# Attention and a gated circular convolution on one core: nearly all products over 64 rows, in couples, with PSUM banks taken in twos

## The chip, the core and the metric

The kernel runs on one core of a Trainium2 chip. The metric is the device time of one execution, in microseconds (us). The core has a matrix engine (TensorE, PE in the profile; its weight loads are shown apart as PEld), a vector engine (DVE), a scalar engine (ACT), GpSimd (POOL), SyncE (SP), which here only issues transfers, and DMA queues. TensorE writes its results to PSUM, which this kernel uses as eight banks of 128 partitions by 512 float32 columns. Every other step reads a bank with ACT or DVE and frees it.

## What is computed

Inputs are q, k, v of 8 batches, 12 heads, 448 positions, 64 features, a projection of 768 by 2304, a filter of 448 by 768 and an output projection of 768 by 768, all float32. Cut to what matters:

```python
scores = q @ k.T / sqrt(64)
e = exp(scores - max); attn = e / (sum(e) + exp(-max) + 1e-9)    # softmax with one more zero score
x = heads side by side (attn @ v)                                # 8 x 448 x 768
x1, x2, x3 = split(x @ w_proj, 3)
x2_conv = irfft(rfft(x2, axis=1) * rfft(filter, axis=0), axis=1) # circular convolution over positions
out = (x1 * x2_conv * x3) @ w_out
```

The kernel doesn't subtract the maximum: it adds 1 to the sum of the exponentials.

## The kernel before

Operands of products are bfloat16, sums are float32 in PSUM. Heads are taken in twos: head pair `hp` of batch `b` is job `i = 6 b + hp`, 48 in all, with one head in partitions 0 to 63 and the other in 64 to 127 of `kT` and `qT`.

**Attention of one head pair** (`attention(i)`, L757). Keys come as four groups of 128. Groups 1 to 3 are ordinary (`scores(t)`, L769): for each head one product over 64 rows, the two heads side by side in the two halves of the array, into two neighbouring PSUM banks (ring `sc`). Group 0 holds the last 64 keys of both heads, zero-padded, and is one product over all 128 rows (L771). ACT takes the exponentials of two banks in one instruction of 128 x 896 (L776), of group 0 in one of 128 x 448 (L782). The values follow: `out_rests` (L791) for group 0, eight small products over 64 rows and 65 columns (the 65th column is all ones and gives the sum), and `out_rest(u)` (L799) for head `u`, twelve over 128 rows and 65 columns. `norm(u)` (L812 to L814) divides on DVE. From batch 1 on, two groups of scores are issued together (`both`), and `out_rests` of the head pair before rides behind one of these jobs (`with_rests`).

**Dense part of a batch** (`dense(b)`, L917). `P` (L973) multiplies four folded copies of the attention's output by the middle third of the projection, six products of 113 outputs by 384 columns into one bank, for four parts by two column halves. `Z` (L1000) is a transform by a small cosine and sine table, one product each. DVE multiplies by the filter's spectrum (L1014, L1020). `I` (L1085) transforms back, four products of 113 columns to a bank. `G` (L1046) makes the two gates, six products over 128 rows and 448 columns for each of six blocks and two gates; ACT copies the first gate (L1058), DVE multiplies it by the second straight from PSUM (L1061). `O` (L1158) is the output projection, six products of 384 columns for each of two column halves of a block of 128 positions; ACT copies each half (L1170), and SP stores the block (L1177). A few full 128-row transposes (L461 to L470, L893) turn inputs of the first two batches and some outputs of the attention.

**Order.** Nothing is ordered while the program runs. At build time every job is given to `Plan` with its engine, a cost, a due time, the tokens that it needs and makes, and the buffers that it takes and gives back. `Plan.run` goes through time with these costs, takes for each free engine the first ready job by due time within a window of 160, and writes the jobs out in that order; each engine then executes its list strictly in order, waiting on semaphores. `spots` (L131) gives out the eight PSUM banks: a couple of neighbouring banks for `sc`, one bank for anything else, with limits in `CAP` (L61): two couples for `sc`, two banks for `op` (values), five for `hy` (all the rest).

Of the kernel before, what the change touches and what calls it, by code (L numbers as in the profile page):

```python
# [41 lines left out]
class Plan:  # L42
# [18 lines left out]
    CAP = {"sc": 2, "op": 2, "hy": 5}  # L61
# [6 lines left out]
    def add(self, eng, cost, want, emit, need=(), make=(), take=(), give=(), dma=0.0, run=256, n=1, after=0.0, begun=(), late=0.0):  # L68
        self.tasks.append((want, len(self.tasks), eng, cost, emit, need, make, take, give, dma, after, run, n, begun, late))

    def run(self):
# [59 lines left out]
        def spots(t):  # L131

            found, count = {}, {}
            for r, tok in t[7]:
# [8 lines left out]
                if r == "sc":  # L143
                    pairs = [(max(until[i], until[i + 1]), i) for i in open_ if i % 2 == 0 and i + 1 in open_]
                    if not pairs:
                        return None
                    i = min(pairs)[1]
                    found[(r, tok)] = (i, i + 1)
                else:
                    if not open_:  # L150
                        return None
                    found[(r, tok)] = (min(open_, key=lambda i: (i < self.LOW, until[i], i)),)
# [28 lines left out]

        while any(queue.values()):
            moved = False
            for e in queue:
                if free[e] > now + 1e-9:
                    continue
                for i, t in enumerate(queue[e][: self.WINDOW]):
                    if ready(t):
                        break
                else:  # L190
                    continue
                del queue[e][i]
# [10 lines left out]
                end = free[e] = now + t[3]  # L203
# [52 lines left out]
def kernel(  # L256
# [16 lines left out]
    EARLY1 = 3.88  # L273
    ATT = [0.66, 29.26, 89.17, 109.42, 158.04, 195.13, 226.82, 281.74]
    SLOT = [2.76, 7.07, 6.79, 7.15, 3.93, 0.11, 6.90, 5.17]
    DENSE = [55.69, 86.75, 129.09, 171.42, 218.23, 260.63, 314.72, 403.09]
    PACE = [1.76, 2.25, 1.51, 1.80, 1.21, 2.06, 0.63, 0.81]
    FOLD = [-0.17, 0.59, -11.07, -14.44, 19.64, 0.57, 9.33, 0.88]
    BPS = 1.39
    RE1 = 9.47  # L280
    WT = 2.21
    FT = 18.26
    HALVED = (2,)
    AHEAD = [0, 0, 44.96, 46.56, 34, 34, 34, 34]
    LEAD = [-5.04, 8.40, 5.33, 27.02]
    LOADS = ((1, 0), (1, 1), ("F", None), (0, None), (2, None), ("O", None))
    LOAD = [36.65, 26.03, 14.30, 37.12, 39.52, 45.70]
    STEP = 3.73
    FOLD0 = (40.54, 56.31, 30.00)
# [34 lines left out]
    er = [const.tile([128, S + REM], BF16, name=f"er{i}") for i in range(2)]  # L324
# [10 lines left out]
    def stage(g, at, n):  # L335
# [6 lines left out]
            "e": 6, "er": 2, "k0": 2, "q0": 2, "u": 1, "w": 1, "xf": 1,  # L342
# [411 lines left out]

    T = {}

    def attention(i):  # L757
# [15 lines left out]
        def exps(t):  # L773
# [6 lines left out]
            else:  # L780
                P["e"][t] = e = er[i % 2]
                nc.scalar.activation(e[:, 0:S], bank(("hy", ("S", i, t)))[:, 0:S], AF.Exp, scale=SCALE)  # L782

        def out_bank(u):
            return bank(("op", (i, u)))[:, 0 : NST * (DH + 1)].rearrange("p (n d) -> p n d", n=NST)

        def out_rests():
            for n in range(NST):
                for u in range(2):
                    c = slice(64 * u, 64 * u + 64)  # L790
                    nc.tensor.matmul(  # L791
                        out_bank(u)[:, n, :], P["e"][0][c, n * 128 : n * 128 + 128], vn[b % 2][c, hp, 3, :],
# [3 lines left out]
        def out_rest(u):  # L796
            for n in range(NST):
                for t in range(3):
                    nc.tensor.matmul(  # L799
                        out_bank(u)[:, n, :],  # L800
                        P["e"][1 + t][:, u * S + n * 128 : u * S + n * 128 + 128],
                        vn[b % 2][:, hp, 4 * u + t, :],
                        start=False,
                        stop=(n == NST - 1 and t == 2),
                    )

        def norm(u):
            op = out_bank(u)
            if ("xb", b) not in W:
                W["xb", b] = xbp.tile([128, NHP, NST, 128], BF16, name="xb")  # L810
            rec = small.tile([128, NST], F32, name="rec")
            nc.vector.tensor_scalar_add(rec, op[:, :, DH], 1.0)  # L812
            nc.vector.reciprocal(rec, rec)
            nc.vector.tensor_tensor(  # L814
                W["xb", b][:, hp, :, 64 * u : 64 * u + 64],
                op[:, :, 0:DH],
                rec[:].unsqueeze(2).to_broadcast([128, NST, DH]),
# [3 lines left out]
        P["scores"], P["rests"] = scores, out_rests  # L821


        host = (2 if b == 0 or i % 2 == 0 else 3) if i else None

        def with_rests(j):
            pb = j // NHP
            vs = [("v", j), ("vr", pb)]
            return dict(
                cost=0.13, emit=T[j]["rests"], need=[("e", j), ("ones", pb % 2), "pads"] + vs, make=[("ER", j)],  # L830
                take=[("op", (j, 0)), ("op", (j, 1))], give=[("er", (j, 0))],
            )

        for t in range(4):
            w = tau(i, t / 4 if i or t else 1.0)
            ex = with_rests(i - 1) if t == host else dict(cost=0.0, emit=lambda: None, need=[], make=[], take=[], give=[])
            if t == 0 or b == 0:

                def one(t=t, ex=ex):
                    scores(t)  # L840
                    ex["emit"]()

                add("PE", (0.4 if t else 0.19) + ex["cost"], w, one,
                    need=[("kT", i), ("qT", i)] + ([("S", i - 1, 2)] if b else []) + ([] if i or t else ["kT0"]) + ex["need"]
                    + ([("S", i, t - 1) if t > 1 else ("S", i - 1, 3)] if t and (i or t > 1) else []),
                    make=[("S", i, t)] + ex["make"], take=[(ring(t), ("S", i, t))] + ex["take"], give=ex["give"])
            elif (3 * i + t) % 2 == 0:

                old = (i, t - 1) if t > 1 else (i - 1, 3)

                def both(pair=(old, (i, t)), ex=ex):
                    for j, n in pair:
                        T[j]["scores"](n)
                    ex["emit"]()

                add("PE", 0.6 + ex["cost"], tau(old[0], old[1] / 4), both,
                    need=[("kT", old[0]), ("qT", old[0]), ("kT", i), ("qT", i)] + ex["need"]
                    + [("S", old[0], old[1] - 1) if old[1] > 1 else ("S", i - 1, 3)],
                    make=[("S",) + old, ("S", i, t)] + ex["make"],
                    take=[("sc", ("S",) + old), ("sc", ("S", i, t))] + ex["take"], give=ex["give"])  # L860
            add("ACT", 0.81 if t else 0.44, w - 1.0, lambda t=t: exps(t), need=[("S", i, t)],
                make=[("e", i)], take=[("e" if t else "er", (i, t))], give=[(ring(t), ("S", i, t))])
        if i == n_batches * NHP - 1:
            ex = with_rests(i)
            add("PE", 0.19 + ex["cost"], tau(i, 1.1), out_rests, need=ex["need"], make=ex["make"], take=ex["take"],
                give=ex["give"])

        w = tau(i + 1, (2 if i % 2 else 1) / 4) + 0.01
        for u in range(2):
            add("PE", 0.385, w + 0.01 * u, lambda u=u: out_rest(u), need=[("ER", i)], make=[("V", i, u)],  # L870
                take=[("op", (i, u))], give=[("e", (i, t)) for t in range(1, 4)])
            add("DVE", 0.8, w - 0.5, lambda u=u: norm(u),
# [455 lines left out]
```

## Time and profile before

The median of three runs is 387.61 us (385.61, 387.61, 388.36). The profile is of one execution.

| of the profiled execution | |
|---|---|
| its own time | 385.59 us |
| span from first to last instruction | 383.8 us |
| granted TensorE clock, mean | 0.993 |
| TensorE matmuls | 3734 in 369.9 us busy |
| DVE | 823 instructions, 276.9 us |
| ACT | 460 instructions, 264.4 us |
| DMA | 58.74 MB, 153 GB/s mean |

The page gives each engine's busy time, the chain of work that ended last, and groups of equal instructions by line (L1046 is line 1046 of the listing). A matmul's row begins when it starts to stream and ends when its result is in PSUM, so rows of consecutive matmuls overlap: the mean of a group is a latency, and the rate is read from the distance of starts. In a timeline the columns are the start, the length of the merged stretch, the engine, the line and the shapes; a bracket tells of idle time before it and of who ended it.

### The profile page before, as it was taken

The numbers are of one execution on the slowest core, as the hardware profiler recorded it, in microseconds if no ns is written. First come the engines' busy times: TensorE is split into PE (matmuls) and PEld (weight loads), VectorE is DVE, ScalarE is ACT, GpSimd is POOL, SyncE is SP. The second block draws the span as 40 slices with busy tenths as digits, with TensorE's granted clock in tenths as the row PEclk, the third lists the DMA queues.
The fourth block names the chain that finished last, engine by engine and source line by source line (L and its number), as shares of the span: only waits on it lengthen the run. The fifth ranks groups of instructions, "written<-read, shape, count | busy, mean of one in ns | idle before, by whom it ended". The sixth has DMA issues, their size and how long they took to land.

```text
span 383.8 us, 9781 instructions
## 1 busy us (share of the span) xinstructions
PE 369.9 (96%) x3734; PEld 236.6 (62%) x3734; DVE 276.9 (72%) x823; ACT 264.4 (69%) x460; POOL 112.3 (29%) x232
## 2 busy tenths in 40 slices
PE   8979999999999999999999999999999999999995
PEld 7656665566665575665665567565675567557652
DVE  6768959955789849984499844995579656971870
ACT  5869688555876878688777777777767775543543
POOL 5678724233552643633553420100000000000000
PEclk9999999999999999999999999999999999999999
DMA  9999999999999999999999965802310042103004
GB/s 212 266 209 244 212 215 213 150 169 191 209 203 206 177 282 244 221 210 230 265 235 138 259 168 122 143 3 82 86 27 2 10 117 70 43 0 125 0 2 164
DMA packets 134574, 58.74 MB, mean 153 GB/s; under 512 B 99389, under 2 KB 130944, under 8 KB 134528
## 3 DMA queue, kind: packets, MB, share of 16 engines
q1 hardware_dynamic: 97104, 48.35, 57.3%
q0 software_dynamic: 37184, 9.54, 27.7%
q8 instruction: 29, 0.48, 0.5%
q10 hardware_dynamic: 240, 0.23, 0.3%
q14 instruction: 17, 0.14, 0.1%
HBM read 43.86 MB, written 11.01 MB: 143 GB/s over the span
## 4 chain that ended last, share of the span: by engine, by line
PE 77%; DVE 13%; DMA 4%; ACT 2%; issue 2%; POOL 1%; SPq 0%; DVEq 0%; ACTq 0%; POOLq 0%
PE psum L1046 23%; PE psum L973 14%; PE psum L1158 14%; PE psum L799 8%; PE psum L769 7%; DMA nat<-in_q_dram 2%; DVE t L1014 2%; PE psum L1000 2%; DMA nat<-in_k_dram 2%; PE psum L1085 2%; PE psum L771 2%; DVE g L1061 2%; DVE yh L1020 1%; DVE cv L1114 1%; ACT e L776 1%
## 5 line engine op out<-in xcount | busy, mean ns | idle before, releaser
L776 ACT ACTIVATE e<-psum 128x896 bf16<-128x896 f32 x144 | 126.1, 925 | 22.7 <-PE psum L769 22.6
L1046 PE MATMUL psum<-xT,wproj_bf 128*128 128x448 bf16 x576 | 121.9, 352 | 0.4 <-DVE g L1061 0.3
L1046 PEld LDWEIGHTS <-wproj_bf 128*128 128x128 bf16 x576 | 53.8, 97 | 44.5 <-issue 2.6
L973 PE MATMUL psum<-wproj_bf,xf 128*113 128x384 bf16 x384 | 69.9, 327 | 0.2 <-DVE kT L480 0.2
L973 PEld LDWEIGHTS <-xf 128*113 128x113 bf16 x384 | 49.5, 132 | 13.0 <-issue 1.4
L1158 PE MATMUL psum<-wout_bf,yT 128*128 128x384 bf16 x288 | 51.9, 327 | 1.3 <-DVE xb L814 0.5
L799 PE MATMUL psum<-vn,e 128*128 128x65 bf16 x1152 | 44.9, 195 | 0.0
L1170 ACT COPY osb<-psum 128x384 f32<-128x384 f32 x56 | 26.1, 483 | 26.8 <-PE psum L1158 26.5
L1058 ACT CAST x<-psum 128x448 bf16<-128x448 f32 x48 | 25.7, 536 | 25.3 <-PE psum L1046 25.2
L814 DVE TENSOR_TENSOR xb<-psum,rec 128x256 bf16<-128x256 f32 x96 | 40.8, 424 | 3.3
L769 PE MATMUL psum<-qT,kT 64*128 64x448 bf16 x288 | 41.4, 358 | 0.0
L799 PEld LDWEIGHTS <-e 128*128 128x128 bf16 x1152 | 39.2, 98 | 2.7
L1158 PEld LDWEIGHTS <-yT 128*128 128x128 bf16 x288 | 27.3, 98 | 21.4 <-issue 2.6
L812 DVE TENSOR_SCALAR rec<-psum 128x4 f32<-128x4 f32 x96 | 14.8, 154 | 34.5 <-PE psum L799 34.4
L598 POOL CAST vn<-nat 128x192 bf16<-128x192 f32 x72 | 27.5, 408 | 40.5 <-DMA nat<-in_v_dram 27.1
L1061 DVE TENSOR_TENSOR g<-x,psum 128x448 bf16<-128x448 bf16 x48 | 29.5, 614 | 10.6 <-PE psum L1046 9.1
L1014 DVE TENSOR_TENSOR t<-xs,hrs 113x768 bf16<-113x768 bf16 (+1 forms) x64 | 35.6, 586 | 1.6 <-ACT xs L1008 1.6
L985 DVE CAST x<-psum 113x384 bf16<-113x384 f32 x32 | 17.6, 552 | 24.8 <-PE psum L973 24.7
L532 POOL DMA_DIRECT2D nat<-in_q_dram x28 | 24.8, 888 | 29.7 <-DMA qT<-nat 17.0
L1008 ACT CAST xs<-psum 113x384 bf16<-113x384 f32 (+1 forms) x64 | 28.2, 495 | 4.1 <-PE psum L1000 3.8
L1094 ACT CAST cr<-psum 128x452 bf16<-128x452 f32 x48 | 25.3, 550 | 7.8 <-PE psum L1085 7.6
L782 ACT ACTIVATE er<-psum 128x448 bf16<-128x448 f32 x48 | 26.9, 560 | 4.4 <-PE psum L771 4.4
(109 smaller groups left out, 444.0 us busy)
## 6 DMA issues: line engine op xcount, KB each, us to landing
nat<-in_k_dram SPq DMA_DIRECT2D x48, 192.0 KB, 5.7
nat<-in_v_dram SPq DMA_DIRECT2D x48, 192.0 KB, 5.2
out_dram<-osb SPq DMA_DIRECT2D x24, 384.0 KB, 3.1
nat<-in_q_dram POOLq DMA_DIRECT2D x20, 168.0 KB, 7.6
nat<-in_q_dram SPq DMA_DIRECT2D x11, 224.0 KB, 7.5
wproj_bf<-in_moe_w_proj_dram POOLq DMA_DIRECT2D x2, 1152.0 KB, 20.4
rests<-in_k_dram SPq DMA_DIRECT2D x8, 192.0 KB, 5.3
rests<-in_v_dram SPq DMA_DIRECT2D x8, 192.0 KB, 7.0
```

The costliest lines, as they stand in the source:

```text
L598: nc.gpsimd.tensor_copy(vn[b % 2][:, hp, 4 * u : 4 * u + 3, 0:DH], sv[:, u])
L769: nc.tensor.matmul(sc[:, u, 0:S], kT[b % 2][c, hp, t, :], qT[b % 2][c, hp, :])
L776: nc.scalar.activation(e[:, 0 : 2 * S].rearrange("p (u n) -> p u n", u=2), pair(("sc", ("S", i, t)))[:, :, 0:S], AF.Exp, scale=SCALE,)
L782: nc.scalar.activation(e[:, 0:S], bank(("hy", ("S", i, t)))[:, 0:S], AF.Exp, scale=SCALE)
L799: nc.tensor.matmul(out_bank(u)[:, n, :], P["e"][1 + t][:, u * S + n * 128 : u * S + n * 128 + 128], vn[b % 2][:, hp, 4 * u + t, :], start= ...
L814: nc.vector.tensor_tensor(W["xb", b][:, hp, :, 64 * u : 64 * u + 64], op[:, :, 0:DH], rec[:].unsqueeze(2).to_broadcast([128, NST, DH]), op ...
L973: nc.tensor.matmul(pps[:FQ, :DCH], W["xf", b][:, pg, kt, 0:FQ], wproj_bf[:, kt, D + ch * DCH : D + (ch + 1) * DCH], start=(kt == 0), stop= ...
L1008: nc.scalar.copy(L["xs", par, ch][:K, pg % 2, :], L["Z", pg, ch][:K, :DCH])
L1014: nc.vector.tensor_tensor(t[:K], L["xs", par, ch][:K], h, op=ALU.mult)
L1046: nc.tensor.matmul(p[:, :S], wproj_bf[:, kt, 2 * part * D + dt * 128 : 2 * part * D + (dt + 1) * 128], xT()[:, kt, 0:S], start=(kt == 0), ...
L1061: nc.vector.tensor_tensor(g[:, dt, :], L["x1", dt], p[:, :S], op=ALU.mult)
L1158: nc.tensor.matmul(ops[:n, :DCH], y[:, dt, 0:n], wout_bf[:, dt, ch * DCH : (ch + 1) * DCH], start=(dt == 0), stop=(dt == NDT - 1),)
```

## The change

Every product over 128 rows of `P`, `Z`, `G`, `I`, `O`, of the values, and from batch 1 on of group 0 of the scores, becomes two products over 64 rows. Two outputs are made at a time, in two neighbouring banks: first the lower rows of one beside the upper rows of the other, for the whole sum (side 0), then the other way round (side 1). Side 1 adds into the banks that side 0 wrote from the other half of the array, so its first matmul waits on a semaphore that side 0's last matmul raises (`mark`, `behind`). The two sides are two jobs for the planner.

```diff
-    CAP = {"sc": 2, "op": 2, "hy": 5}
+    REACH = 9.60
+    TURN = 0.1
+    CLOSE = 0.12
+    PAIRS = ("sc", "op", "tw")
+    CAP = {"sc": 2, "op": 2, "tw": 4, "hy": 4}
...
-                if r == "sc":
+                if r in self.PAIRS:
                     pairs = [(max(until[i], until[i + 1]), i) for i in open_ if i % 2 == 0 and i + 1 in open_]
...
+                near = at = None
                 for i, t in enumerate(queue[e][: self.WINDOW]):
-                    if ready(t):
+                    if near is not None and t[0] > queue[e][near][0] + self.REACH:
                         break
-                else:
+                    if not ready(t):
+                        continue
+                    if prev is not None and t[16] in prev[6]:
+                        near = i if near is None else near
+                        continue
+                    at = i
+                    break
...
-                end = free[e] = now + t[3]
+                end = now + t[3]
+                if e == "PE":
+                    if close:
+                        end += self.CLOSE
+                    if t[15] != bool(prev and prev[15]):
+                        end += self.TURN
...
+    def mark(last):
+
+        last.then_inc(half_done, 1)
+        halves_done[0] += 1
+        tc.add_to_no_dep_group(f"half {halves_done[0]}", last.ins)
+        tc.no_tile_sem_insts.add(last.ins.name)
+        return halves_done[0]
+
+    def behind(first, count):
+
+        first.wait_op(half_done, count, "sem-ge")
...
+        def couples(units, side, part=slice(None), last=None):
+
+            first, second = units[side][part], units[1 - side][part]
+            whole = units[0]
+            for n, two in enumerate(zip(first, second)):
+                for low, (to, w, x) in enumerate(two):
+                    c = slice(64 * low, min(64 * low + 64, w.shape[0]))
+                    now = nc.tensor.matmul(
+                        to, w[c], x[c], start=(side == 0 and n == 0 and not part.start),
+                        stop=(side == 1 and n == len(whole) - 1), skip_group_check=True,
+                    )
+                    if last is not None:
+                        behind(now, last)
+                        last = None
+            return mark(now) if not side and part.stop is None else None
+
+        def twin(key, cost, w, units, need, make, extra=(), give=(), split=None):
...
+                add("PE", cost * (1.0 if split is None else (split[1], 1 - split[1])[j]), w + 0.3 * j, lambda part=part: L.update({half: couples(L[key](), 0, part)}),
+                    need=need if not j else [half + (j - 1,), *split[2]], make=[half + (j,)], take=[tw] if not j else (),
+                    row=True)
...
+            add("PE", cost, w + 0.02 + 0.3 * (len(parts) - 1), lambda: couples(L[key](), 1, last=L[half]), need=[last], make=make, give=give, row=True, apart=last)
```

`REACH` makes the planner look for another ready job to put between the two sides; where there is none it puts side 1 directly behind side 0 and counts `CLOSE` for it. `TURN` is counted where a job over 64 rows follows one over 128 or the other way round.

The rest follows from taking outputs in twos. The values of both heads are one job pair: `way` (`out_rests` and side 0) and `values(1)`; no job carries `out_rests` along any more, and no two groups of scores are tied together. `norm` takes both heads at once, group 0 of two head pairs gets one exponential of 128 x 896 (`two_exps`), and ACT copies both banks of a `Z`, an `I` and an `O` in one instruction. `P` keeps one copy by ACT and one by DVE. Both gates of a block are one twin, so the first gate's copy comes after the second side too:

```diff
-            if part == 0:
-                add("ACT", 0.43, w, lambda: gate_back(dt, 0), need=[("G", b, dt, 0)], make=[("x1", b, dt)],
-                    take=[x1], give=[hy])
...
+            tw = twin(tuple(keys), 1.135, w, lambda banks: gate(dt, banks),
...
+            add("ACT", 0.43, w, lambda: gate_back(dt, 0), need=[keys[0]], make=[("x1", b, dt)], take=[x1], give=[tw])
+            add("DVE", 0.55, w - 0.5, lambda: gate_back(dt, 1), need=[keys[1], ("x1", b, dt), "half"],
+                make=[("g", b, dt // 2)], take=[("g", b)], give=[tw, x1])
...
-        def project_back(st, ch):
-            n = 128 if st < 3 or b % 2 else REM
...
+        def project_back(st, tw):
+            L["os", st] = otp.tile([128, D], F32, name="osb")
+            nc.scalar.copy(L["os", st][:].rearrange("p (u n) -> p u n", u=2), pair(tw)[:, :, :DCH])
```

The first two blocks of `O` have side 0 in two parts, four couples that need two thirds of the gated rows and two that need the last third. The due times (`ATT`, `SLOT`, `DENSE`, `PACE`, `FOLD`, `LOAD` and others) all have new values. In the built program TensorE has 6479 matmuls in place of 3734, 6164 of them over 64 rows, where 672 were before; ACT has 364 instructions in place of 469, DVE 687 in place of 831.

## The prediction

> **What bounds the kernel now.** I read the page first, then the waits, then timelines of TensorE.
>
> ```profile
> PE 369.9 (96%) x3734; PEld 236.6 (62%) x3734; DVE 276.9 (72%) x823; ACT 264.4 (69%) x460; POOL 112.3 (29%) x232
> ...
> PE 77%; DVE 13%; DMA 4%; ACT 2%; issue 2%; POOL 1%; SPq 0%; DVEq 0%; ACTq 0%; POOLq 0%
> ```
>
> TensorE is busy nearly throughout and carries 77% of the chain that ended last, so time is won or lost on TensorE. Its busy figure hides short holes, since a row lasts until its result has landed. So I take rates from starts. The timeline of TensorE inside batches 4 and 5:
>
> ```profile
> 240.04 0.55 PE L769 MATMUL psum<-qT,kT 64*128 64x448 bf16 x4
> 240.43 0.28 PE L791 MATMUL psum<-vn,er 64*128 64x65 bf16 x8
> 240.64 1.19 PE L973 MATMUL psum<-wproj_bf,xf 128*113 128x384 bf16 x6
> 241.66 0.92 PE L799 MATMUL psum<-vn,e 128*128 128x65 bf16 x24
> ...
> 244.92 0.49 PE L1000 MATMUL psum<-x,ft 113*112 113x384 bf16 x2
> 245.25 1.30 PE L1046 MATMUL psum<-xT,wproj_bf 128*128 128x448 bf16 x6
> 246.38 0.35 PE L771 MATMUL psum<-qT,kT 128*128 128x448 bf16 x1
> 246.57 2.43 PE L1046 MATMUL psum<-xT,wproj_bf 128*128 128x448 bf16 x12
> 248.94 0.55 PE L769 MATMUL psum<-qT,kT 64*128 64x448 bf16 x4
> ```
>
> Three things are to be seen. (a) Full rows: 245.25 to 246.38 is six matmuls of 448 columns, 0.189 each; 244.92 to 245.25 is two of 384, 0.163 each. (b) Half rows in couples: four L769 take 0.39, so a couple costs 0.195, the same as one full matmul and not twice it. Eight L791 take 0.21, which with the next point leaves 0.12, or 0.030 a couple; 24 full ones of L799 take 0.76, or 0.032 each. (c) Changing the height costs: 246.57 to 248.94 is 2.37 for twelve matmuls that need 12 x 0.189 = 2.27, so 0.10 is lost before the 64-row scores. The other way, L791's four couples need 0.12 of their 0.21, so 0.09 is lost. The first 128-row matmul after it can lose a little more for a weight load that nothing hid: six L973 take 1.02 where 6 x 0.162 = 0.97 is due.
>
> Real stalls are few. The waits of TensorE:
>
> ```profile
> PE psum L893 <- DVE xb L814: 1.7, 2, 1.0
> PE psum L463 <- POOL k L421: 1.7, 1, 1.7
> PE psum L1085 <- DVE xb L814: 1.1, 2, 0.9
> ```
>
> These are the largest, totals in us. By start distances I count about 13 us of stalls: 6.6 in the first 43 us and 6.4 after.
>
> **What the change takes away.** Streaming stays as it is: a couple of 64-row matmuls does the work of one 128-row matmul at the same rate (b), with twice the instructions. Counted in the order of the two programs, changes of height fall from 160 to 71, because transposes, the filter's spectrum and batch 0's group 0 stay full. 89 x 0.096 (mean of 0.10 and 0.09) is 8.5 us, and some forty hidden weight loads of 0.01 to 0.05 make it **-9 us**. Small values at 0.030 and not 0.032 give 1152 x 0.001, **-1 us**. DVE loses 48 of 96 sets of small reciprocal steps, and ACT a quarter of its instructions; both have slack (72% and 69%), so I give that nothing. Were TensorE quicker than them in a stage, it would be worth at most the 6.4 us of stalls.
>
> **What it adds: TensorE waits for itself.** Each of 233 second sides waits until the last matmul of its first side has landed. Queued behind it is everything that TensorE does next, so the wait can't be stepped around. No such wait exists in the trace, so I price it by two neighbours. A row's latency beyond its streaming:
>
> ```profile
> L1046 PE MATMUL psum<-xT,wproj_bf 128*128 128x448 bf16 x576 | 121.9, 352 | 0.4 <-DVE g L1061 0.3
> ...
> L973 PE MATMUL psum<-wproj_bf,xf 128*113 128x384 bf16 x384 | 69.9, 327 | 0.2 <-DVE kT L480 0.2
> ```
>
> 352 - 189 and 327 - 162 give 0.164. A hop on a semaphore: DVE's L1061 ends at 212.68 and the L1046 that waits for it starts at 212.74, 0.05 to 0.06; from TensorE to ACT, L1158's stretch ends at 379.35 and the copy starts at 379.38, 0.03. So side 1 starts 0.19 to 0.22 after side 0 has stopped streaming; I take 0.216, as the hop that ends at TensorE is the nearest. What lies between the sides in the program's order pays for it. Summing the pitches of the matmuls in between: 34 second sides have nothing between them and their first, 34 x 0.216 = 7.3 us; 116 have one short job, 0.184 on average, mostly one couple of scores or of `Z`, 116 x 0.032 = 3.7; 83 have more and lose nothing. That makes **+11 us**. It is steep: at 0.18 it is 6.6 us, at 0.25 it is 16. The floor is that of a change of height, 0.096, which also waits for the array to empty: 3.3 us. After a wait that bites, the partner's weight load is exposed, 0.01 as after the stall at 64.61 (next start 0.067 on, not 0.056) to 0.05: 150 of them, **+1 us** (0 to 5).
>
> **Banks in twos.** Eight single banks become four couples. An exponential holds its couple for 0.35 (the matmul) + 0.03 + 0.925 + 0.05 = 1.36 us from the start of the scores. In the new order 36 places give a bank back to TensorE with less matmul work in between than such a chain needs, 7.8 us short in sum (3.3 of it in batch 5, where scores follow each other closely); the same count for the order before gives 2 places and 0.35 us. The self-waits stretch the same distances, so I take less than half, **+3 us**, with 0 and 8 as ends.
>
> **The end.** The last stage runs on DVE's chain; TensorE then works off `O`:
>
> ```profile
> 371.05 2.11 PE L1158 MATMUL psum<-wout_bf,yT 128*128 128x384 bf16 x12
> 373.32 2.12 PE L1158 MATMUL psum<-wout_bf,yT 128*128 128x384 bf16 x12 [0.15 <-DVE yT L1129]
> ```
>
> After the last gate TensorE has twelve matmuls of 0.162 in hand, then waits 0.3 for DVE, then 36 more. Changed, it has 8 couples (1.30) in hand, while the first gate's copy (0.53, earlier done one matmul group sooner), the multiply (0.61) and `yT` (0.55) with three hops must pass: about 2.0. After that 40 couples are left where 36 matmuls were, 0.65 more, and the last copy is of 768 columns, some 0.3 more than the 0.48 of 384. The earlier return of 0.3 set against this, **+1 us** (0.5 to 3).
>
> **Sum.** 385.6 - 9 - 1 + 11 + 1 + 3 + 1 = 391.6 on the profiled execution's own time. The median of the runs lies 2.0 above that execution, so the forecast is **394 us**.
>
> A rule that speaks against the change, beside the row: couples of L791 start 0.030 apart, so 65 columns over 64 rows cost no more than over 128. The Trainium skill (TensorEngine Tiling (Array Packing), Instruction Overhead) gives each matmul about 60 cycles of overhead and advises against tiling where a dimension is already small; at its 2.4 GHz that would be an estimated 0.025 per matmul, hence 0.050 a couple, and with 28 couples for each of 48 head pairs some 27 us more. The row decides, so the sum has none of it; but it shows only eight in a row, where the change issues up to 32.
>
> **Rivals.**
>
> *Faster: the self-wait is cheap.* If the array's emptying is all that side 1 waits for (0.096, 3.3 us in sum), and the other engines' lighter load makes up for banks in twos: 385.6 - 9 - 1 + 3.3 + 1 = 380, or 382 as a median. For it: four sides in five have something between them, and a change of height empties the array in 0.096. Against it: a semaphore has to go out and back, and every hop in the trace takes 0.03 or more after a row's end at 0.164. The change breaks even when waits, banks and end together cost 10 us, which is at about 0.17 a wait. Chance 0.27.
>
> *Slower: banks in twos rule.* If the bank shortfall comes in full (8) and the self-waits and the end at their upper values (16, 5 and 3): 385.6 - 10 + 32 = 408 at the worst, some 403 with half of the excess. Chance 0.12.
>
> *Slower: instructions come too slowly.* Weight loads and matmuls are 12,958 where 7468 were. The densest long stretches of the trace, near 8 to 25 us, bring 256 matmuls in 17.3 us, which shows no more than one per 0.068 sustained; shorter bursts reach one per 0.031 over 32. If 0.031 were the limit for the values' 2688 matmuls, they would take 83 us where 40 are due; with half of it covered by instructions queued ahead, +20 us, so 414. The trace has no hole that looks like it. The Trainium skill (TensorE: Matmul & The Clock Gate, Wait — 56ns, not 53.3ns?) states about 62 ns of microcode per matmul where hardware decode is off; 6479 of these would be an estimated 402 us by themselves, and no run here shows which setting holds. Chance 0.08.
>
> *It doesn't do what it says: couples that add into PSUM don't run side by side.* L769 writes without adding; L791 adds only over 65 columns. If couples of 384 and 448 columns went one after the other, some 290 us of streaming would double. Chance 0.03.
>
> **How the numbers follow.** The forecast's own case, 388 to 400, has 0.50. One per cent of 387.6, about what a measurement can tell, sets the bounds 383.7 and 391.5. Faster: three quarters of the first rival and a tail of the forecast, 0.22. Same: the rest of that rival and over a quarter of the forecast, 0.21. Slower: 0.57. The range 381 to 406 leaves out some 0.08 at the faster end and 0.12 above.
>
> **What would show it.** In the changed profile a couple of 448 columns starts every 0.19 and one of 65 every 0.030 (else the last two rivals). Side 1's first matmul, directly behind side 0's last, starts about 0.40 after it with 448 columns (0.189 + 0.216); 0.29 would speak for the cheap wait. Changes of height lose 0.09 to 0.10 at 71 places. Waits of TensorE on ACT's L814 (exponentials) would show the banks, and `yT` the end. I am wrong if starts keep step through the second sides, or if stalls in the first 43 us, which I left as they are, move by several us.

## The result and the profile after

The changed kernel takes 407.81 us (median of four runs, 405.21 to 416.09) where the kernel before takes 387.84 (385.61 to 388.36). The ratio is 1.051, with a 95% interval of 1.045 to 1.057: slower by 20 us. The forecast was 394 with a range up to 406. The execution first profiled was a disturbed one (416.09 us, mean granted clock 0.970), so the lines below are from a second execution of the same kernel: 411.47 us, span 409.6, clock 0.984. They lie some 4 us above the median. Below, a self-wait is the wait of a side 1 for its own side 0, and a hole is a stretch in which TensorE stands still.

From the page of the changed kernel: busy time of the engines, the granted clock in 40 slices, the queue that brings TensorE its instructions (packets, MB, share), and the chain that ended last:

```profile
PE 377.3 (92%) x6479; PEld 266.8 (65%) x6479; DVE 261.1 (64%) x679; ACT 259.6 (63%) x355; POOL 111.3 (27%) x231
...
PEclk9996999999999999999999899999999999999998
...
q8 instruction: 50, 0.82, 0.9%
...
PE 71%; DMA 10%; DVE 10%; ACT 3%; issue 3%; POOL 1%; SPq 1%; ACTq 0%; DVEq 0%; POOLq 0%
```

TensorE is busy for 7 us more, but its share falls from 96% to 92%: the time went mostly into idle time of the engine that bounds the kernel. DMA carries 10% of the chain where it carried 4%. The line of q8 has its counterpart on the page of before, which the prediction didn't look at:

```profile
q8 instruction: 29, 0.48, 0.5%
```

The groups of `G` and of the values in the changed kernel (line, engine, shapes, count, busy and mean ns, idle before):

```profile
L1021 PE MATMUL psum<-xT,wproj_bf 64*128 64x448 bf16 x1152 | 125.3, 351 | 0.8 <-ACT er L822 0.4
...
L846 PE MATMUL psum<-vn,e 64*128 64x65 bf16 x2304 | 54.7, 191 | 2.2 <-issue 1.4
```

1152 matmuls over 64 rows are busy for 125.3 us where 576 over 128 rows took 121.9. Couples do run side by side, and streaming costs what it did. The timeline of TensorE late in the attention, beside which the first timeline of before can be read:

```profile
227.66 0.37 PE L807 MATMUL psum<-qT,kT 64*128 64x448 bf16 x2
227.90 0.36 PE L874 MATMUL psum<-qT,kT 64*128 64x448 bf16 x2
228.08 0.36 PE L807 MATMUL psum<-qT,kT 64*128 64x448 bf16 x2
228.27 0.19 PE L834 MATMUL psum<-vn,er 64*128 64x65 bf16 x1
228.92 0.27 PE L834 MATMUL psum<-vn,er 64*128 64x65 bf16 x6 [0.46 <-DVE g L1133]
232.00 0.20 PE L834 MATMUL psum<-vn,er 64*128 64x65 bf16 x1 [2.81 <-issue]
232.00 0.58 PE L846 MATMUL psum<-vn,e 64*128 64x65 bf16 x24
232.39 0.38 PE L807 MATMUL psum<-qT,kT 64*128 64x448 bf16 x2
```

Couples of scores start 0.18 to 0.24 apart, as forecast; 24 small values stream in 0.39. But TensorE stands still for 2.81 us in the middle of eight small products of one job, and no semaphore released it: "issue". No such line was among the largest waits of before. Those of the changed kernel (TensorE's line, who released it, total us, times, longest):

```profile
PE psum L937 <- DVE xb L864: 3.6, 2, 3.4
PE psum L834 <- issue: 2.8, 1, 2.8
PE psum L492 <- POOL q L449: 2.1, 4, 0.9
PE psum L483 <- DVE xb L864: 1.8, 1, 1.8
PE psum L1021 <- issue: 1.6, 2, 0.8
PE psum L846 <- issue: 1.4, 2, 0.9
PE psum L807 <- ACT x L1063: 1.4, 1, 1.4
PE psum L834 <- ACT e L814: 1.3, 2, 0.7
PE psum L1021 <- DVE yT L1196: 1.3, 1, 1.3
```

The self-waits aren't in this list at all: a start 0.22 after the end of streaming leaves only 0.06 of idle time behind the row before, whose latency reaches 351 - 189 = 0.16 beyond its streaming. They must be taken from starts. The end of the kernel shows one:

```profile
391.79 2.69 PE L1021 MATMUL psum<-xT,wproj_bf 64*128 64x448 bf16 x24
394.29 1.48 PE L1021 MATMUL psum<-wout_bf,yT 64*128 64x384 bf16 x16
397.05 2.77 PE L1021 MATMUL psum<-wout_bf,yT 64*128 64x384 bf16 x32 [1.28 <-DVE yT L1196]
```

391.79 to 394.29 is 2.50 for twelve couples, and 12 x 0.189 = 2.27; the 0.23 left is side 1 of a gate, directly behind its side 0.

Going through all start distances of TensorE in this way, with everything beyond the streaming put down to its cause, gives (us; a self-wait bites where TensorE really stood for it):

| lost by TensorE | before (span 383.8) | after (span 409.6) | difference |
|---|---|---|---|
| changes of height, 160 and 71 | 15.3 | 6.8 | -8.5 |
| self-waits that bite, 137 | 0 | 13.5 | +13.5 |
| no releaser | 0.4 | 7.9 | +7.5 |
| waiting for ACT | 0.4 | 7.9 | +7.5 |
| waiting for DVE | 8.8 | 10.2 | +1.4 |
| waiting itself for a transfer (`kT`, `xT`) | 0 | 1.5 | +1.5 |
| from the last matmul's start to the end | 4.8 | 6.2 | +1.4 |
| spread over many small differences | | | +1.5 |
| span | 383.8 | 409.6 | +25.8 |

Of the 10.2 for DVE, 3.4 is one wait at 31.55 us: DVE, which works in order, had stood idle for 4.1 us until the filter's transfer (`filt`) landed, and the `xb` that TensorE needed came behind that. In the kernel before, DVE never waited for `filt`.

**The holes without a releaser.** Counting TensorE's instructions, weight loads among them, in the order of their starts, six holes after 50 us stand at nearly the same place of a block of 256: at numbers that leave 190, 186, 184, 182, 182 and 180 when divided by 256 (the count is good to about 2). Five are "issue". The first of the six, at 57.11, is the 1.4 us under `ACT x L1063` above, since that semaphore had come shortly before. Queue q8 brings packets of 16 KB, 50 of them for 12,958 instructions: one packet is 256 instructions. Late in the kernel, with few transfers left, packets start when TensorE is near instruction 160 of a block (0.6 us before it to 1.4 after), so the boundary at which a packet is asked for is put there. Three of the holes with their packets (worked out from the trace's start and length of each packet; us):

```
boundary before passed   packet starts   packet landed   TensorE goes on   hole
186.40                   190.85          192.01          193.30            0.9
200.56                   205.08          206.17          207.62            1.0
221.97                   228.60          230.38          232.00            2.8
```

A packet is asked for when TensorE passes the boundary before, starts with a delay while other transfers run, takes about 1.2 us, and TensorE goes on 1.3 to 1.7 us after it has landed, in all six holes. In the kernel before, between 50 and 250 us, packets start 2.6 us after the boundary on average, at most 4.0, and blocks of 256 instructions last 12.5 us (median; the shortest 10.2), so every packet landed at least 6.5 us before the next boundary. In the changed kernel, in the same stretch, blocks last 7.4 us (the shortest 3.9), and packets start 3.8 us after the boundary on average, up to 7.0. The six holes cost 7.6 us. The wait at 31.55 stands near the same place in its block, but its packet had landed at 26.61, so it isn't one of them.

### The profile page after: what moved, and what is told of

Same layout as the page of the kernel before. It is cut to its first block, busy times and chain, and to the rows that moved or that the text cites. A ratio compares the mean times of both kernels' runs of the same rounds, so it can differ in the third digit from the quotient of the medians.

```text
span 414.2 us, 14970 instructions
## 1 busy us (share of the span) xinstructions
PE 382.5 (92%) x6479; PEld 270.9 (65%) x6479; DVE 261.7 (63%) x679; ACT 259.8 (63%) x355; POOL 112.1 (27%) x231
## 4 chain that ended last, share of the span: by engine, by line
PE 72%; DMA 9%; ACT 7%; DVE 6%; issue 4%; POOL 1%; SPq 1%; DVEq 0%; ACTq 0%; POOLq 0%
PE psum L1021 53%; PE psum L846 7%; PE psum L807 5%; ACT e L814 4%; DMA filt<-in_moe_filter_fft_dram 2%; DMA xT<-xb 2%; DMA kT<-nat 2%; DMA nat<-in_v_dram 2%; PE psum L874 2%; PE psum L834 1%; DMA nat<-in_k_dram 1%; DVE cv L1181 1%; PE psum L1288 1%; PE psum L937 1%; DVE g L1133 1%
## 5 line engine op out<-in xcount | busy, mean ns | idle before, releaser
L1021 PE MATMUL psum<-xT,wproj_bf 64*128 64x448 bf16 x1152 | 128.9, 358 | 0.2
L1021 PEld LDWEIGHTS <-wproj_bf 64*128 64x128 bf16 x1152 | 66.2, 96 | 40.4 <-issue 6.6
L1021 PE MATMUL psum<-wproj_bf,xf 64*113 64x384 bf16 x768 | 73.5, 324 | 0.9 <-issue 0.5
L1021 PEld LDWEIGHTS <-xf 64*113 64x113 bf16 x768 | 57.7, 128 | 9.9 <-issue 2.7
L846 PE MATMUL psum<-vn,e 64*128 64x65 bf16 x2304 | 56.2, 194 | 7.3 <-issue 6.6
L1021 PE MATMUL psum<-wout_bf,yT 64*128 64x384 bf16 x576 | 54.6, 323 | 1.4 <-DVE yT L1196 1.3
L846 PEld LDWEIGHTS <-e 64*128 64x128 bf16 x2304 | 46.9, 96 | 13.4 <-issue 10.2
L1021 PEld LDWEIGHTS <-yT 64*128 64x128 bf16 x576 | 31.0, 94 | 17.4 <-DVE yT L1196 2.0
L864 DVE TENSOR_TENSOR xb<-psum,rec 128x512 bf16<-128x512 f32 x48 | 33.2, 691 | 1.7
L1082 ACT CAST xs<-psum 113x768 bf16<-113x768 f32 (+1 forms) x32 | 24.9, 803 | 5.7 <-PE psum L1021 3.3
```

What stands on the lines that cost most here:

```text
L846: now = nc.tensor.matmul(out_bank(u)[:, n, :], P["e"][1 + t][c, u * S + n * 128 : u * S + n * 128 + 128], vn[b % 2][c, hp, 4 * u + t, :], ...
L864: nc.vector.tensor_tensor(W["xb", b][:, hp].rearrange("p n (u d) -> p u n d", u=2), op[:, :, :, 0:DH], rec[:].unsqueeze(3).to_broadcast([1 ...
L1021: now = nc.tensor.matmul(to, w[c], x[c], start=(side == 0 and n == 0 and not part.start), stop=(side == 1 and n == len(whole) - 1), skip_g ...
L1082: nc.scalar.copy(L["xs", par, ch][:K], pair(tw)[:K, :, :DCH])
```

## Experiments

Two theories were open. One: TensorE waits for its instructions, which is a rival that the prediction priced as a rate of issue and not as late packets. The other: banks in twos and the new order starve TensorE through ACT and DVE. The self-wait was common to both.

**A second execution of the changed kernel**, unchanged.

> The changed kernel once more, for a second trace. If the holes without a releaser come from TensorE running out of fetched instructions, they stand again before instructions whose number is 180 to 184 modulo 256, while transfers are busy (before 250 us), each about 1.5 us after a packet of 16 KB has landed, though not all at the same blocks. If they were chance disturbances of that one execution (clock 0.97), this one, at about 405 to 408 us, has none. Second sides directly behind first ones start 0.40 us after the last 448-column matmul in either case.

411.47 us, the profile shown above. Which boundaries are late differs between executions: the execution first profiled has its holes of over 2 us at 31.89, 198.32 and 229.90, this one at 232.00. The place in the block stays (178 to 190), and in the first execution too TensorE goes on 1.2 to 1.7 us after the packet has landed, at seven holes with 10 us of idle time. That execution has one more long wait, of 4.3 us, for DVE's gate: DVE had waited for the transfer `xT<-xb`, which landed 8.4 us after its issue.

**No self-waits.** Side 1 takes the same halves as side 0, so each sum holds one half of its rows twice and the other not at all:

```diff
-            first, second = units[side][part], units[1 - side][part]
+            first, second = units[0][part], units[1][part]
...
-                        behind(now, last)
...
-                        u = low ^ side
+                        u = low
```

> Side 1 takes the same halves as side 0 (each output adds the same 64 rows twice, so values differ from the reference), and nothing waits on its own first side; order, instructions, streaming and banks stay. If the self-waits cost what the trace shows (139 of them, 13.8 us), it takes 407.8 - 14 = 394 us, 392 to 397. If they only cover waits for banks or for instructions that come late, those grow in their place and it takes 400 to 406. If self-waits were the whole loss, it would be at or below 388.

403.11 us (398.61 to 404.48), ratio 1.041 (1.034 to 1.049). So 4.7 us of the 13.5 came back. Its profile has 8.3 us without a releaser, and waits for DVE have grown from 10.2 to 14.6. Of these, 4.7 is one wait behind `xT<-xb`, at the same instruction as in the first execution of the changed kernel, so it can't be put down to the edit. That a self-wait that is taken away lets TensorE reach the next late packet or late buffer sooner fits the numbers, but isn't separated here from such differences between executions.

**More instructions in the kernel before.** The products of `G`, `P` and `O` are cut into columns, four quarters (7622 matmuls) or two halves (5030), all over 128 rows, with no self-wait and the old order and banks:

```diff
-                nc.tensor.matmul(
-                    p[:, :S],
+                for z in range(4):
+                    zs = slice(z * (S // 4), (z + 1) * (S // 4))
+                    nc.tensor.matmul(
+                        p[:, zs],
```

> The kernel before with every matmul of G, P and O cut into four of a quarter of the columns: 7622 matmuls in place of 3734, no second sides, no banks in twos, the same order. 3888 more starts at 0.0025 us add 10 us of streaming, so 398 if the number of instructions costs nothing else. If instruction fetch binds while transfers are busy, holes at block boundaries come on top, 3 to 10 us: 401 to 408, all of them before 250 us.

> As the one with quarters, but halves: 5030 matmuls, 1296 more starts, 3 us of streaming, 391 us. With 9.8 us to a block of 256 instructions on average the fetch should still keep up: no hole, or one or two of under 1 us. If holes are as many as with quarters, it is not the rate of instructions that makes them.

Halves: 390.61 us in one execution, no hole at a boundary. Quarters: 409.63 (407.88 to 412.54), ratio 1.062 (1.055 to 1.069). That looks like a proof of the first theory and isn't one. The page of the quarters, with the weight loads of `P` (L975) and `O` (L1164), and the largest wait without a releaser:

```profile
PE 393.7 (97%) x7622; PEld 354.5 (87%) x7622; DVE 276.4 (68%) x823; ACT 264.8 (65%) x460; POOL 114.2 (28%) x232
...
q8 instruction: 59, 0.97, 1.0%
...
L975 PEld LDWEIGHTS <-xf 128*113 128x113 bf16 x1536 | 86.8, 134 | 2.9 <-issue 1.1
...
L1164 PEld LDWEIGHTS <-yT 128*128 128x128 bf16 x1152 | 51.1, 98 | 4.2 <-issue 3.4
```

```profile
PE psum L1164 <- issue: 1.3, 3, 0.9
```

TensorE's share is 97% and holes at boundaries sum to about 2 us, in spite of 59 packets. The time went into the matmuls: a quarter of `O` (96 columns) starts every 0.042 and one of `G` (112) every 0.049, near a quarter of 0.162 and 0.189, but one of `P` (96) only every 0.053. `P` alone has weights of 113 columns, and their loads are the longer ones (134 ns against 98); 96 columns no longer hide them. 1536 x (0.053 - 0.0405) is 19 us, and `G` and `O` add 2304 x 0.002 + 1152 x 0.0015 = 6: all of the excess, where about 10 had been allowed. The Trainium skill (TensorE: Matmul & The Clock Gate, Weight-path perf modes) has its fast weight load only for weights of 128 columns, which agrees with 134 against 98. Packets alone don't stall TensorE: here, between 50 and 250 us, blocks last 6.5 us, never under 5.4, and packets start at most 5.8 after the boundary. It takes short blocks together with late packets.

**Quiet queues.** If other traffic makes the packets late, less of it should bring them in time. The transposing transfers of q and k of batches 2 to 7 are left out, in the changed kernel and in the one before (their scores then use the operands of batches 0 and 1 again; `k_turn` is emptied like `q_turn`):

```diff
         def q_turn(gs=gs, st=st):
-            nc.sync.dma_start(
-                qT[b % 2][:, gs, st * SP : (st + 1) * SP], qn[:, st, 128 * gs.start : 128 * gs.stop], transpose=True
-            )
+            pass
```

> The changed kernel with the same transfers left out. If late instruction fetch behind busy DMA queues costs what the two traces show after 60 us (6 to 7 us of holes at block boundaries, 1 to 3 us of halved clock behind the long ones, 1 us waiting for kT), it takes 396 to 400 us and has no such hole after 60 us. If the holes only stand where TensorE would otherwise wait for banks or DVE, it stays at 404 to 408 with longer waits on ACT and DVE.

> The kernel before without the 28 and 16 transposing transfers of q and k of batches 2 to 7 (these batches' scores use what batches 0 and 1 left in qT and kT); everything else stays. TensorE has no hole at a block boundary here and hardly waits for transfers, so every theory expects 383 to 387 us, within 1% of the kernel before.

Changed: 399.93 us (398.61 to 402.92), ratio 1.033 (1.024 to 1.041). Before: 384.13 (382.83 to 386.77), 0.995 (0.991 to 0.998). The changed kernel gains 7.9 by the medians (7.0 by the ratios), the kernel before 2.3 against its 386.39 in the same comparison (2.1 by the ratio). The page of the changed kernel without these transfers, and a stretch like the one of the 2.81 us hole:

```profile
q1 hardware_dynamic: 61136, 39.50, 37.6%
q0 software_dynamic: 37184, 9.54, 24.4%
q8 instruction: 50, 0.82, 0.8%
```

```profile
221.08 0.50 PE L828 MATMUL psum<-vn,er 64*128 64x65 bf16 x8
221.41 0.55 PE L840 MATMUL psum<-vn,e 64*128 64x65 bf16 x24
221.93 0.36 PE L801 MATMUL psum<-qT,kT 64*128 64x448 bf16 x2
222.12 0.56 PE L840 MATMUL psum<-vn,e 64*128 64x65 bf16 x24
222.74 0.37 PE L801 MATMUL psum<-qT,kT 64*128 64x448 bf16 x2
```

Still 50 packets, but q1 has 61,136 packets in place of 97,104. Between 50 and 250 us instruction packets start 2.0 us after the boundary on average in place of 3.8, and after 60 us no hole behind a late packet is left; three before that remain, 3.5 us of idle time. The eight small products that were torn apart run through in 0.33. The same instructions, in the same order, no longer stall there: this settles that the holes after 60 us are packets held up by other transfers. It doesn't settle how much of the 7.9 is theirs. The idle time behind late packets falls from 7.2 to 3.5 us between the two profiles, but TensorE's own wait for `kT` (1.1) goes as well, and DVE waits 1.9 us for `xT<-xb` in place of 8.9.

**Quiet queues and no self-waits**, the two edits together.

> As the one before, and side 1 takes the same halves as side 0 without a wait (each output adds the same 64 rows twice). If fetch and self-waits add up (10 and 4.7 us), 392 to 395 us. What is then left over the kernel before is banks in twos and the order. If the two hide each other, 397 to 403.

390.09 us (388.68 to 393.08), ratio 1.009 (1.005 to 1.014). Now the self-waits are worth 9.8 us (from 399.93), twice what they were with busy queues. And 6.0 are left over the kernel before with quiet queues (384.13), though this one changes height 89 times less. Its waits:

```profile
PE psum L483 <- DVE xb L854: 2.6, 1, 2.6
PE psum L801 <- ACT e L808: 2.1, 6, 0.6
PE psum L1006 <- DVE g L1115: 2.0, 2, 1.0
PE psum L828 <- ACT e L808: 1.6, 3, 0.7
```

By start distances TensorE waits 11.2 us for ACT and 11.8 for DVE, 23.0 in all. With quiet queues the kernel before waits 10.3 for DVE and next to nothing for ACT. 8.5 gained on height, some 13 given back at the other engines and about 1.5 at the end make the 6.0.

**The new order and banks, with products over 128 rows again.** Jobs, order, banks and ACT's and DVE's work are the changed kernel's; side 0 makes one output, side 1 the other, each over all rows:

```diff
-            first, second = units[side][part], units[1 - side][part]
...
+            for n, (to, w, x) in enumerate(units[side][part]):
+                nc.tensor.matmul(to, w, x, ...)
```

> The changed kernel's order and banks in twos, but every product of the change again over 128 rows (side 0 makes one output, side 1 the other, no self-wait): 3733 matmuls, 336 changes of height in place of 71, 25 us more. Without self-waits (4.7) and fetch holes (12 in all) it takes 407.8 - 16.7 + 25.4 = 416 us, with no hole at a block boundary. If the number of instructions had no part in the holes, 428. If banks in twos and the order cost nothing, it is the kernel before plus 176 changes of height: 403.

409.04 us in one execution, span 407.2. It has as few instructions as before and no self-wait, and no hole at a boundary after 20 us:

```profile
PE 390.4 (96%) x3733; PEld 237.4 (58%) x3733; DVE 260.2 (64%) x679; ACT 259.1 (64%) x355; POOL 112.2 (28%) x231
...
q8 instruction: 29, 0.48, 0.5%
```

```profile
PE psum L926 <- DVE xb L857: 2.3, 2, 2.1
PE psum L1006 <- DVE yT L1178: 1.3, 1, 1.3
```

Its 23.4 us over before come apart as 16.9 for 176 more changes of height (336 x 0.096 = 32.2), 2.8 more waiting for ACT and DVE (12.0 in place of 9.2), 1.4 more at the end, and 2.3 left, which the clock can account for: it was near half speed from about 33 to 41 us, and its mean allows up to 3.8 ((1 - 0.984) x 407.2 against (1 - 0.993) x 383.8). So the order and the banks cost little while TensorE is slow, in this one execution; the 13 us of the run with quiet queues and no self-waits appear when it is quick.

**Shorter exponentials.** If the exponentials held the banks for too long, halving them should free TensorE. From batch 1 on, the exponential covers one bank of its two, so the other head's weights stay stale; with quiet queues, in the kernel without self-waits and in the one before:

```diff
+                m = 2 if b == 0 else 1
...
-                    e[:, 0 : 2 * S].rearrange("p (u n) -> p u n", u=2), pair(("sc", ("S", i, t)))[:, :, 0:S], AF.Exp,
+                    e[:, 0 : m * S].rearrange("p (u n) -> p u n", u=m), pair(("sc", ("S", i, t)))[:, 0:m, 0:S], AF.Exp,
```

> The run with transposes left out and both sides alike, and from batch 1 on each exponential of two banks does only the first (448 of 896 columns; the other half keeps an older head pair's values). Its couple of banks comes back 0.37 us sooner. If what is left over the kernel before (390.1 against 384.1) stands where scores wait for exponentials, the 11 us of waits on ACT shrink to under 3 and it takes 380 to 383. If it is the fixed order and DVE, 388 to 390.

> The same halved exponentials in the kernel before with the transposes left out. TensorE waits on ACT for under 1 us there, so all theories expect 383 to 385 us, as without the halving (384.1). A gain of several us would say that the exponentials bind in both kernels, and the run beside this one shows nothing of banks in twos.

387.69 us (386.8 to 392.2), ratio 1.003 (0.998 to 1.007), and 383.07 (382.76 to 384.69), 0.992 (0.987 to 0.997). The gap shrinks from 6.0 to 4.6. TensorE's waits for ACT fall from 11.2 to 6.6, but those for DVE rise from 11.8 to 12.7. The 1.4 between 6.0 and 4.6 is within the intervals of the four ratios (about 2 us each), so that exponentials explain any of the 6 isn't shown; the hoped-for larger share didn't come.

**More between the sides.** The planner lets a side 1 be ready only 0.23 us after its side 0, so that it looks harder for something to put in between:

```diff
+            if len(t) > 16 and t[16] in when and when[t[16]][0] + 0.23 > now + 1e-9:
+                return False
```

> The changed kernel, computing everything, but the planner holds a second side ready only 0.23 us after its first side's end, so it puts more work in between or counts the wait. By the order, 64 second sides fall short and not 150, by 4.7 us and not 11. Were self-waits additive, it would gain 6 us: 402. Since leaving all of them out gained 4.7 with transfers running, I expect 403 to 406, holes at block boundaries as before. Above 408 the new order costs more than the waits.

410.90 us (407.43 to 416.37), ratio 1.059 (1.050 to 1.067). Self-waits fall from 13.5 to 5.8 us, as meant, and the kernel is no faster: waits for ACT go from 7.9 to 15.0, for DVE from 10.2 to 17.4. What was put between the sides seems to have been taken from where it was needed.

**Fewer changes of height without any couples.** In the kernel before, the planner prefers a ready job of the same height among those due within 3 us:

```diff
+                    if e == "PE" and t[15] != prev:
+                        near = i if near is None else near
+                        continue
```

> The kernel before, products as they were; only the planner, when TensorE comes free, prefers a ready job of the same height whose due time is within 3 us of the first ready one's. Changes of height fall from 160 to 150: 10 x 0.096 = 1 us, so 385.5 beside 386.5, if the changed order costs nothing. A loss of over 1 us would say that the order written with these due times has no slack for even that.

392.39 us (390.52 to 394.51), ratio 1.013 (1.008 to 1.018): ten changes fewer (about 1 us) and 5 us more in all. The waits:

```profile
PE psum L1059 <- DVE xb L827: 2.9, 2, 2.5
PE psum L782 <- DVE xT L915: 2.1, 1, 2.1
PE psum L483 <- POOL q L440: 1.6, 3, 0.8
PE psum L1059 <- DVE g L1074: 1.6, 1, 1.6
```

Waits for DVE are 15.4 us in place of 8.8. The order of before had no slack for this rearrangement.

No kernel tried computes everything and beats the one before.

## Why the prediction was wrong

**What held.** The sign, and the sizes of what TensorE does by itself. Couples of 448 columns start 0.189 apart, of 384 every 0.162: they run side by side, and the rival that they don't is out. Changes of height fell to 71 at 0.092 to 0.096 each, -8.5 us (-9 forecast). A side 1 directly behind its side 0 starts 0.216 to 0.220 after the end of streaming, and 0.406 after its last start with 448 columns, where 0.216 and about 0.40 were forecast from a row's latency and a hop. That ruled out the cheap self-wait (0.096), the most likely rival. 137 self-waits bite and cost 13.5, the exposed weight loads with them, where 150 at 11 + 1 were forecast; the spread of what lies between the sides is a little less kind than the count by the planner's order. Small couples start 0.0315 apart, so the values gain nothing (-1 forecast), and the rule of 60 cycles overhead per matmul is not borne out either: it would have shown 0.050. The same couples, two matmuls in 0.0315, leave no room for the 62 ns of microcode for each that the prediction quotes; it said that no run shows which setting holds, but its own row of 0.030 a couple already did.

**The step that failed** is in the third rival: "The trace has no hole that looks like it." It took slow instructions as a rate of issue and looked for that rate in the densest bursts. TensorE issues fast enough; it runs out of instructions at the end of a block of 256 when the next packet is late. No hole was to be seen in the trace of before because after 50 us packets came 6.5 us early or more, and before that still 2.1. But the margin could be read there: 29 packets on q8, how late each started (up to 4.0 us), and how long the shortest blocks lasted (10.2, and 8.0 in the first 50 us). Halving these puts a block of 4 to 5 us against a packet that needs up to 4.0 + 1.1 + 1.4 = 6.5. In the changed kernel packets even started up to 7.0 late; why later than before stays open. The missing term measured 7.6 us at six boundaries. With it the sum of 391.6 on the profiled execution would have been about 399. Late packets can also cost clock: it is at half speed for 3.4 us from 232.8, right after the longest hole, worth at most 1.7 us. The clock's mean allows 3.8 us more loss than before in all, but the other halved stretches, at 31.4 and 38.2 us, go with waits for DVE.

The Trainium skill (Runtime: NRT & Kernel Launch, Instruction fetch mechanics) says that instructions come in blocks of 16 KiB, 256 of them, which the sequencer fetches through a DMA queue of its own while it executes the current block, and that the cost is "mostly hidden". The packets of 16 KB agree. Hidden holds for the kernel before and, after 60 us, for the quiet one, and not for the changed one with busy queues, where one crossing cost 2.8 us. The same skill (TensorE: Matmul & The Clock Gate, What's actually happening) halves the clock after at least one idle window of about 3.4 us. The halved stretches in the profiles of both kernels do last 3.4 us, but no wholly idle window came before them: in the 3.4 us before the one at 232.8 TensorE was busy for 0.8 us, and in the kernel before, ahead of one at 27.2, for 1.8.

**Banks in twos, and the order, under-sized.** +3 was forecast (0 to 8). TensorE waits 18.1 us for ACT and DVE where it waited 9.2, and 1.5 of that is a late packet under ACT's name: +7.4. Not all of this is banks. 3.4 is the wait behind `filt` at 31.55, which leaves +4.0; with it stalls in the first 43 us are about 9.3 in this profile where they were 6.3, a sign of being wrong that the prediction had named. DVE also stood idle for `xT<-xb` for 8.9 us where it stood 0.5 before, and how much of that TensorE's waits for DVE hold isn't separated. The count behind the 3 looked at which banks come back late, and "I take less than half" because self-waits stretch the distances. That reason fits the run with 128-row products, where TensorE is slow too and the waits grow by 2.8. The miss was to treat the term as its own. What TensorE saves elsewhere makes it meet ACT and DVE sooner. When self-waits and most late packets are gone the same waits grow to 23.0, so part of the savings is spent there. How the 6.0 us left then divide between the exponentials' hold on the banks, the banks of the rest and the fixed order stays open, as no kernel had the one without the other.

**The end**, +1 forecast: TensorE stands about 1.1 us longer for `yT` (by starts 1.46 in place of 0.32, counted above with DVE), and the last matmul's start lies 1.4 further from the end. That is about +2.5, inside the 0.5 to 3.

**What wasn't costed** and is small: TensorE's own waits for transfers, 1.5 us, nearly all of it `DMA kT<-nat` at one place.

The forecast sum, -9 - 1 + 11 + 1 + 3 + 1 = +6, becomes -8.5 + 0 + 13.5 + 7.4 + 1.4 + 7.6 = +21.4, the 1.4 being the end without its wait for `yT`. The 1.5 for transfers and 2.9 in small pieces make up the 25.8 measured in this execution; at the median it is 20. The range ended at 406 because the only rivals beyond it had a chance of 0.12, 0.08 and 0.03, and the second was priced on the wrong mechanism. The measured time does lie where the first of them, "banks in twos rule", put it (403 to 408), but that is luck: it has no late packets, and it reached 408 with self-waits, weight loads and the end all at their upper values.

## What to carry to other kernels

Before doubling the instructions of the engine that bounds a kernel, look up the engine's instruction packets: how long its shortest blocks of 256 last, and how late packets start behind the other transfers; if the first comes near the second plus some 2.5 us (1.1 of transfer and 1.4 until TensorE went on), expect holes. Trading one stall of an engine (a change of height) for another (waiting for its own result) is only a gain if the wait is cheaper than 89 x 0.096 / 137 = 0.06 us each; here it was 0.10 on average and 0.22 uncovered. In an order that is fixed at build time, time saved on the busiest engine is partly handed to the next wait, so savings need not add: leaving the self-waits out gained 4.7 us with busy queues and 9.8 with quiet ones.

## What the runs showed of the hardware that wasn't expected

- TensorE has about one block of 256 instructions in hand: when a boundary is passed, the packet for the instructions from the next boundary on is asked for, and when it is late TensorE stands still at 178 to 190 of the block until 1.2 to 1.7 us after it has landed.
- An instruction packet waits among the data transfers: in the changed kernel up to 7.0 us from the boundary to its start while q1 and q0 are busy, at most about 1.4 us after 250 us, when the big loads are done.
- Weights of 113 columns load more slowly than weights of 128 (134 ns against 98): matmuls of 96 columns start 0.053 us apart with the former and 0.042 with the latter. With 384 columns the difference is hidden, both start 0.162 apart.
- A semaphore wait of TensorE on itself costs 0.22 us beyond streaming, and the 0.06 of idle time that it leaves doesn't appear among the waits of the profile.
